# Decode attention beside a gated feed-forward: each tile of keys, values and query weights loaded as two halves from two queues

## The chip, the cores and the metric

The kernel runs on one core of one Trainium2 chip. The metric is device time in microseconds (us) of one execution, as the median of several runs. The core has five engines, each with its own instruction stream: TensorE (PE in the profile; PEld is its loading of weights), VectorE (DVE), ScalarE (ACT), GpSimd (POOL) and SyncE (SP). Memory transfers are issued from the instruction stream of an engine and carried out by 16 DMA engines. The engines wait for one another, and for transfers, by semaphores; a transfer adds 16 to its semaphore when it is complete.

## The reference

For one new token in each of four sequences, the output mixes an attention block over a cache of 4096 positions with a gated feed-forward block. All arrays are float32.

```python
# x: 4 x 1 x 512; k_cache, v_cache: 4 x 32 x 4096 x 128; wq: 512 x 4096; wo: 4096 x 512
# w_gate, w_up: 512 x 1792; w_down: 1792 x 512; gate_w: 512
g = sigmoid((x * gate_w).sum(-1, keepdims=True))

q = (x @ wq).reshape(4, 1, 32, 128).transpose(0, 2, 1, 3)
scores = einsum("bhqd,bhkd->bhqk", q, k_cache) * 128 ** -0.5
p = softmax(scores)
o = einsum("bhqk,bhkd->bhqd", p, v_cache)
a = o.transpose(0, 2, 1, 3).reshape(4, 1, 4096) @ wo

b = (gelu(x @ w_gate) * (x @ w_up)) @ w_down
return g * a + (1 - g) * b
```

Each element of the two caches is used once; together they are 536.9 MB of the 564.7 MB that the kernel reads.

## The kernel before, in words

**Tiles.** The caches are cut into 32 tiles each (`NT`), one for each group of four heads and each sequence. A tile is 128 partitions x 16384 floats: `heads` (L121) gives each partition 128 successive positions of one head, one contiguous row of 64 KB. There are two buffers for keys, `K[0]` and `K[1]`, and one for values, `V`. Before the first tile of values, `V` holds the queries' weights `wq`, also as 128 rows of 64 KB.

**Loads.** The helper `load` (L125) issues every transfer from SyncE, so that they all stand in one queue in the order in which SyncE reaches them. At the start these are `wq`, `x`, the gate's weights and the first two tiles of keys. Then SyncE waits for `wq_done` (L293), the end of the query projection, and loads the first values. After that (L309 to L314) it waits in turn for `summed[i]`, when VectorE has read the tile of keys `i` for the last time, and loads keys `i + 2`; and for `at_values[i]`, when TensorE has read values `i`, and loads values `i + 1`. The last values, tile 31 (`L1`), are loaded at L323, behind the two up projections' weights `w_gate` and `w_up` (L320), which go to the buffer `K[0]`, and ahead of `w_down` and part of `wo`, which go to `K[1]`. The last 14 of 32 row blocks of `wo` (`got_w`, L362) take the place of the up weights; SyncE issues them when `have_hT` (L355) says that those are no longer needed.

**Keys.** For each tile `keys(i)` (L266) runs on VectorE: the product of the whole tile with the query `QB` in place (L269), the sum over each 128 (L271), and three short instructions (L273 to L275) that give the negated maximum `NM`.

**ScalarE.** In tile `i` (L299 to L308) ScalarE takes the next query from PSUM (L221), spreads the one after it (L215), computes the exponentials with `weights(i)` (L283: four activations, one per head), waits for `at_values[i]`, and copies the weighted sum from PSUM to `o` (L308).

**TensorE.** One loop over 31 tiles (L253): the spreading of a query, the softmax's totals (L224), a wait for the values' semaphore `sem_v`, from which it takes 16 off again, 64 groups of matmuls against `V` (L231), and the turning of the result (L237). The last tile is written out after the loop (L380 to L391). In between stand the up projections (L338), for which the order of the instructions puts `got_up` ahead of the last values. After it come the down projection and the output projection (L376, L428), and the result is stored (L433).

**Semaphores of the loads.** The two of the keys, `sem_k`, count up over the kernel (16 for each tile that has landed in that buffer); the one of the values is counted back by TensorE.

Of the kernel before, what the change touches and what calls it, by code (L numbers as in the profile page):

```python
# [34 lines left out]
def tile_gated_mix(ctx: ExitStack, tc: tile.TileContext, x, kc, vc, wq, wo, w_gate, w_up, w_down, gate_w, out):  # L35
    nc = tc.nc
# [4 lines left out]
    KC = DM // P  # L41
# [3 lines left out]
    TW = R * D  # L45
    NG = H // HT
    NT = NG * B
# [32 lines left out]
    K = [kv.tile([P, TW], F32, name=f"k{s}") for s in range(2)]  # L80
    V = kv.tile([P, TW], F32, name="v")
# [25 lines left out]
    def semaphore(name):  # L107
        counters.append(ctx.enter_context(nc.semaphore(name)))
        return counters[-1]

    ctx.enter_context(tc.tile_critical(sync_engine=mybir.EngineType.SP))
    SP = Line(nc.sync, None)
    PE = Line(nc.tensor, semaphore("pe"))
    DV = Line(nc.vector, semaphore("dv"))
    AC = Line(nc.scalar, semaphore("ac"))
    PL = Line(nc.gpsimd, semaphore("pl"))
    token_a, token_d = semaphore("token_a"), semaphore("token_d")
    sem_k = [semaphore(f"sem_k{s}") for s in range(2)]
    sem_v = semaphore("sem_v")

    def heads(src, i):  # L121
        g, b = divmod(i, B)
        return src[b, HT * g:HT * g + HT].rearrange("h (p r) d -> (h p) (r d)", p=PH)

    def load(dst, src, sem=None, name=None):  # L125
        sem = sem or semaphore(name)
        nc.sync.dma_start(dst, src).then_inc(sem, 16)  # L127
        return sem, 16

    def load_k(i):  # L130
        load(K[i % 2], heads(kc, i), sem_k[i % 2])

    def load_v(i):
        load(V, heads(vc, i), sem_v)

    got_q = load(V, wq.rearrange("(p c) n -> p (c n)", c=KC), name="got_q")
    x_sb = o[:B]
    got_x = load(x_sb, x.rearrange("b s d -> (b s) d"), name="got_x")
    gw = gs[:B]
    got_g = load(gw, gate_w.rearrange("(o n) -> o n", o=1).to_broadcast([B, DM]), name="got_g")  # L140
    load_k(0)
    load_k(1)

    p0 = PL.do(nc.gpsimd.memset(ident, 0.0))
    PL.wait(p0)
# [56 lines left out]
    for s in range(2):  # L202
# [3 lines left out]
        wq_done = PE.do(u)  # L206
# [6 lines left out]
    def spread_query(i):  # L213
        g, b = divmod(i, B)
        return nc.scalar.activation(QX, QT[:, b, HT * g:HT * g + HT, None].to_broadcast([P, HT, PH]), AF.Copy)  # L215

    def spread():
        return nc.tensor.matmul(qp[:, :D], QX.rearrange("p h k -> p (h k)"), ident, start=True, stop=True)  # L218

    def take_query(i):  # L220
        return AC.do(nc.scalar.activation(QB[i % 2], qp[:, :D], AF.Copy, scale=scale))  # L221

    def totals():
        return nc.tensor.matmul(tot, ones, RS, start=True, stop=True)  # L224

    def values():
        p = PM.rearrange("p r h -> p (r h)")
        n = R // RJ
        for j in range(n):
            c = j % 4  # L230
            t = nc.tensor.matmul(po[32 * c:32 * c + M], p[:, j * M:(j + 1) * M], V[:, j * RJ * D:(j + 1) * RJ * D],  # L231
                                 start=j < 4, stop=j >= n - 4)
        return t

    def turn():
        for j in range(RJ):
            t = nc.tensor.matmul(quo, o[:, j * D:(j + 1) * D], pick[:, j, :], start=j == 0, stop=j == RJ - 1)  # L237
        return t
# [6 lines left out]
    have_QB = {0: take_query(0)}  # L245
    have_QX = AC.do(spread_query(1))

    L1 = NT - 1
# [4 lines left out]
    with nc.tensor.Fori(0, L1):  # L253
        spread().then_inc(PE.sem, 1)
        nc.tensor.wait_ge(token_a, 2).then_inc(token_a, -2)
        nc.tensor.wait_ge(token_d, 1).then_inc(token_d, -1)  # L256
        totals()
        nc.tensor.wait_ge(sem_v, 16).then_inc(sem_v, -16)  # L258
        values().then_inc(PE.sem, 1)
        nc.tensor.wait_ge(token_a, 1).then_inc(token_a, -1)  # L260
        turn().then_inc(PE.sem, 1)
    PE.n += 3 * L1

    summed, have_nm, have_OT = {}, {}, {}

    def keys(i):  # L266
        k = K[i % 2].rearrange("p (r d) -> p r d", d=D)
        DV.wait((sem_k[i % 2], 16 * (i // 2 + 1)), have_QB[i])
        DV.wait(DV.do(nc.vector.tensor_tensor(k, k, QB[i % 2][:, None, :].to_broadcast([P, R, D]), op=OP.mult)))  # L269
        sc = SC[i % 2]  # L270
        summed[i] = DV.do(nc.vector.tensor_reduce(sc, k, axis=AX.X, op=OP.add))  # L271
        DV.wait(summed[i])
        DV.wait(DV.do(nc.vector.tensor_reduce(m1, sc, axis=AX.X, op=OP.max)))  # L273
        DV.wait(DV.do(nc.vector.transpose(mt, m1.to_broadcast([P, 32]))))  # L274
        have_nm[i] = DV.do(nc.vector.tensor_reduce(NM[i % 2], mt, axis=AX.X, op=OP.max, negate=True))  # L275

    def divide(i, at):
        g, b = divmod(i, B)
        DV.wait(at)
        DV.wait(DV.do(nc.vector.reciprocal(ri, tot)))  # L280
        return nc.vector.tensor_tensor(OT[:, b, HT * g:HT * g + HT], quo, ri, op=OP.mult)

    def weights(i):  # L283
        AC.wait(have_nm[i])
        if i:
            AC.wait(at_values[i - 1])
        for h in range(HT):
            s = slice(h * PH, (h + 1) * PH)
            t = nc.scalar.activation(PM[s, :, h], SC[i % 2][s, :], AF.Exp, bias=NM[i % 2][s, :], scale=1.0,  # L289
                                     accum_out=RS[s, h:h + 1])  # L290
        return t

    SP.wait(wq_done)  # L293
    load_v(0)
    for i in range(NT):
        keys(i)
        if i > 0:
            divide(i - 1, at_turn[i - 1]).then_inc(token_d, 1)
        if i < L1:  # L299
            AC.wait(at_spread[i])  # L300
            have_QB[i + 1] = take_query(i + 1)
            if i + 2 < NT:
                spread_query(i + 2).then_inc(token_a, 1)
            else:
                nc.scalar.sem_inc(token_a, 1)
            weights(i).then_inc(token_a, 1)
            AC.wait(at_values[i])
            nc.scalar.activation(o, po, AF.Copy).then_inc(token_a, 1)  # L308
        if i + 2 < NT:  # L309
            SP.wait(summed[i])  # L310
            load_k(i + 2)
        if i + 1 < L1:
            SP.wait(at_values[i])
            load_v(i + 1)  # L314
    have_PM = AC.do(weights(L1))

    f, down = K[0], K[1]
# [2 lines left out]
    got_up = [load(f[:, s * KC * F:(s + 1) * KC * F], a.rearrange("(p c) n -> p (c n)", c=KC), name=f"got_up{s}")  # L320
              for s, a in enumerate((w_gate, w_up))]
    SP.wait(at_values[L1 - 1])
    load_v(L1)  # L323
    SP.wait(summed[L1])
    got_down = load(down[:, :DR * DM], w_down.rearrange("(p i) n -> p (i n)", i=DR), name="got_down")
    got_wo = [load(down[:, (DR + r0) * DM:(DR + r1) * DM], wo_rows[:, r0 * DM:r1 * DM], name=f"got_wo{r0}")
# [34 lines left out]
    for n in PIECES:  # L361
        got_w.append(load(f[:, r0 * DM:(r0 + n) * DM], wo_rows[:, (W1 + r0) * DM:(W1 + r0 + n) * DM],  # L362
                          name=f"got_w{r0}"))
# [16 lines left out]
    PE.wait(have_PM)  # L380
    nc.tensor.wait_ge(token_d, 1)
    totals()
    nc.tensor.wait_ge(sem_v, 16)
    t = PE.do(values())
    AC.wait(t)
    have_o = AC.do(nc.scalar.activation(o, po, AF.Copy))
# [30 lines left out]
    i = 0  # L417
# [42 lines left out]
```

## Time and profile before

| | us |
|---|---|
| median of 3 runs | 1311.73 |
| lowest, highest | 1311.70, 1312.22 |
| the profiled execution, its own time | 1312.45 |
| its span in the profile | 1310.7 |
| busy in it: VectorE | 1142.5 (87%) |
| busy in it: TensorE matmul, weight load | 390.0 (30%), 136.1 (10%) |
| busy in it: ScalarE | 108.7 (8%) |

The profile describes one execution. A page line of a group of instructions reads: line of the kernel, engine, operation, output<-input with sizes, count | busy us, mean ns of one | idle us of the engine just before them, and what ended most of that idle time. In a timeline the columns are the start in us, the duration in us, engine, line, operation, and in brackets the idle time before it with what ended it; "SPq" is SyncE's issuing of a transfer. In the table of stretches the columns are the stretch, its length, the busy us (and the count of instructions) of PE, PEld, DVE, ACT and POOL, TensorE's granted clock, the share of the 16 DMA engines' time that packets fill, and GB/s. Packets are counted to the stretch in which they begin, so that short stretches scatter. The line of digits "DMA" on the page gives that share in tenths, 9 being 90% or more, over 40 equal slices of the span.

### The profile page before, as it was taken

To read this page: it belongs to the slowest core of one execution; us is meant where nothing else is said; L and a number is where in the kernel's file an instruction comes from. 1 tells how busy PE (TensorE), PEld (TensorE's weight loads), DVE (VectorE), ACT (ScalarE), POOL (GpSimd) and SP (SyncE) were. 2 spreads that over 40 slices of the span, in tenths; PEclk is the share of its full clock that TensorE was granted. 3 is DMA by queue.
4 is the path that set the end of the run, shared out by engine and by line. 5 is a ranking of instruction groups with operands and counts; after the bars stand their busy time and mean duration, and the time that the engine had idled before them with its cause. 6 is when DMAs were issued, how large, how long until landed. Compare 5 with 4: busy or idle time off the path is not lost.

```text
span 1310.7 us, 6525 instructions
## 1 busy us (share of the span) xinstructions
PE 390.0 (30%) x2766; PEld 136.1 (10%) x2766; DVE 1142.5 (87%) x263; ACT 108.7 (8%) x360; POOL 0.7 (0%) x6
## 2 busy tenths in 40 slices
PE   2132123333213333312333321233231133332147
PEld 0010001111001111000111100011010011100012
DVE  1799999999989899998989989998998999899850
ACT  0000111000000000000000000000000000000010
POOL 0000000000000000000000000000000000000000
PEclk9665566666556666656666655666655666665578
DMA  9999999999999999999999999999999999999998
GB/s 417 416 447 428 436 443 422 444 420 448 426 438 438 426 444 420 448 422 442 436 428 444 420 444 424 440 438 428 446 420 444 422 442 436 428 448 418 434 430 342
DMA packets 10846, 564.80 MB, mean 431 GB/s; under 512 B 1212, under 2 KB 1228, under 8 KB 1620
## 3 DMA queue, kind: packets, MB, share of 16 engines
q1 hardware_dynamic: 10836, 564.69, 99.5%
q8 instruction: 4, 0.07, 0.0%
q14 instruction: 6, 0.05, 0.0%
HBM read 564.67 MB, written 0.01 MB: 431 GB/s over the span
## 4 chain that ended last, share of the span: by engine, by line
DMA 51%; DVE 48%; PE 1%; issue 0%; SPq 0%; ACT 0%
DMA k<-in_A_k_cache 45%; DVE k L269 24%; DVE SC L271 24%; DMA k<-in_B_w_up 3%; DMA k<-in_A_wo 3%; PE bank L338 0%; PE bank L428 0%; SPq L127 0%; DVE m L273 0%; DVE k L354 0%; DVE mt L274 0%; DVE k L351 0%; DVE k L352 0%; DVE nm L275 0%; ACT k L349 0%
## 5 line engine op out<-in xcount | busy, mean ns | idle before, releaser
L269 DVE TENSOR_TENSOR k<-k,QB 128x16384 f32<-128x16384 f32 x32 | 551.2, 17225 | 82.6 <-DMA k<-in_A_k_cache 82.6
L271 DVE TENSOR_REDUCE SC<-k 128x128 f32<-128x16384 f32 x32 | 551.0, 17220 | 1.1
L231 PE MATMUL bank<-v,PM 128*16 128x512 f32 x2048 | 294.7, 740 | 569.8 <-PEq L258 555.7
L231 PEld LDWEIGHTS bank<-v,PM 128*16 128x16 f32 x2048 | 69.4, 113 | 768.5 <-issue 754.3
L224 PE MATMUL bank<-RS,ones 128*128 128x4 f32 x64 | 17.7, 347 | 288.0 <-PEq L256 288.0
L308 ACT ACTIVATE o<-bank 128x512 f32<-128x512 f32 x31 | 18.5, 597 | 869.2 <-PE bank L231 869.2
L289 ACT ACTIVATE PM<-SC,nm 32x128 f32<-32x128 f32 x128 | 66.0, 516 | 200.9 <-DVE nm L275 199.4
L224 PEld LDWEIGHTS bank<-RS,ones 128*128 128x128 f32 x64 | 15.8, 306 | 294.3 <-issue 294.3
L237 PE MATMUL bank<-pick,o 128*128 128x4 f32 x256 | 32.9, 252 | 25.1 <-PEq L260 25.1
L237 PEld LDWEIGHTS bank<-pick,o 128*128 128x128 f32 x256 | 31.0, 191 | 53.6 <-issue 52.7
L280 DVE RECIPROCAL ri<-bank 128x4 f32<-128x4 f32 x32 | 5.5, 173 | 22.5 <-PE bank L237 22.5
L289 ACT ACTIVATION_READ_ACCUMULATOR PM<-SC,nm 32x1 f32 x128 | 25.1, 196 | 0.0
L167 DVE COPY xT<-bank 128x32 f32<-128x32 f32 x4 | 0.5, 182 | 21.5 <-PE bank L163 21.5
L218 PE MATMUL bank<-ident,QX 128*128 128x128 f32 x64 | 15.0, 316 | 1.5 <-ACT QX L215 1.5
L221 ACT ACTIVATE QB<-bank 128x128 f32<-128x128 f32 x32 | 8.9, 278 | 47.3 <-PE bank L218 47.3
L432 DVE COPY res<-bank 128x128 f32<-128x128 f32 x1 | 0.3, 292 | 12.5 <-PE bank L428 12.5
L273 DVE TENSOR_REDUCE m<-SC 128x1 f32<-128x128 f32 x32 | 9.2, 286 | 1.1
L215 ACT ACTIVATE QX<-QT 128x128 f32<-128x128 f32 x32 | 9.9, 308 | 2.4 <-DVE QT L209 1.6
L209 DVE COPY QT<-bank 128x16 f32<-128x16 f32 x8 | 0.9, 180 | 10.5 <-PE bank L205 10.5
L218 PEld LDWEIGHTS bank<-ident,QX 128*128 128x128 f32 x64 | 9.7, 192 | 1.9 <-ACT QX L215 1.1
L193 PE MATMUL bank<-v,xT 128*32 128x512 f32 x64 | 9.5, 760 | 0.0
L338 PE MATMUL bank<-k,xT 128*32 128x448 f32 x64 | 8.1, 659 | 2.6 <-DMA k<-in_B_w_up 2.6
(57 smaller groups left out, 63.5 us busy)
## 6 DMA issues: line engine op xcount, KB each, us to landing
k<-in_B_w_gate SPq DMA_DIRECT2D x1, 3584.0 KB, 31.9
k<-in_B_w_up SPq DMA_DIRECT2D x1, 3584.0 KB, 40.0
k<-in_B_w_down SPq DMA_DIRECT2D x1, 3584.0 KB, 29.5
k<-in_A_wo SPq DMA_DIRECT2D x1, 2560.0 KB, 35.2
k<-in_A_wo SPq DMA_DIRECT2D x1, 2048.0 KB, 39.6
k<-in_A_wo SPq DMA_DIRECT2D x2, 1024.0 KB, 33.5
k<-in_A_wo SPq DMA_DIRECT2D x1, 768.0 KB, 35.9
k<-in_A_k_cache SPq DMA_DIRECT2D x32, 42.7
```

The costliest lines, as they stand in the source:

```text
L193: t = nc.tensor.matmul(PO[s][32 * j:32 * j + 32], xT[:, c, :], w[:, c, n0:n0 + HB * D], start=c == 0, stop=c == KC - 1)
L215: return nc.scalar.activation(QX, QT[:, b, HT * g:HT * g + HT, None].to_broadcast([P, HT, PH]), AF.Copy)
L218: return nc.tensor.matmul(qp[:, :D], QX.rearrange("p h k -> p (h k)"), ident, start=True, stop=True)
L221: return AC.do(nc.scalar.activation(QB[i % 2], qp[:, :D], AF.Copy, scale=scale))
L224: return nc.tensor.matmul(tot, ones, RS, start=True, stop=True)
L231: t = nc.tensor.matmul(po[32 * c:32 * c + M], p[:, j * M:(j + 1) * M], V[:, j * RJ * D:(j + 1) * RJ * D], start=j < 4, stop=j >= n - 4)
L237: t = nc.tensor.matmul(quo, o[:, j * D:(j + 1) * D], pick[:, j, :], start=j == 0, stop=j == RJ - 1)
L269: DV.wait(DV.do(nc.vector.tensor_tensor(k, k, QB[i % 2][:, None, :].to_broadcast([P, R, D]), op=OP.mult)))
L271: summed[i] = DV.do(nc.vector.tensor_reduce(sc, k, axis=AX.X, op=OP.add))
L273: DV.wait(DV.do(nc.vector.tensor_reduce(m1, sc, axis=AX.X, op=OP.max)))
L289: t = nc.scalar.activation(PM[s, :, h], SC[i % 2][s, :], AF.Exp, bias=NM[i % 2][s, :], scale=1.0, accum_out=RS[s, h:h + 1])
L308: nc.scalar.activation(o, po, AF.Copy).then_inc(token_a, 1)
```

## The change

Each tile of keys and values, and the queries' weights, is loaded by two transfers into the same buffer: the left half of each of the 128 rows (8192 floats, 32 KB) from SyncE, the right half from ScalarE. Both add to the same semaphore, so the waits go from 16 to 32. ScalarE's half of the first values waits for `wq_done` like SyncE's. In tile `i`, ScalarE issues its half of keys `i + 2` behind the exponentials of tile `i`, and its half of values `i + 1` behind the copy to `o`. Its half of the last values is thereby issued in the loop (`i = 30`), while SyncE's stays behind the up weights at L323 of the kernel before. All other loads stay with SyncE.

```diff
--- before.py
+++ after.py
@@ -127,19 +127,26 @@
         nc.sync.dma_start(dst, src).then_inc(sem, 16)
         return sem, 16
 
-    def load_k(i):
-        load(K[i % 2], heads(kc, i), sem_k[i % 2])
-
-    def load_v(i):
-        load(V, heads(vc, i), sem_v)
-
-    got_q = load(V, wq.rearrange("(p c) n -> p (c n)", c=KC), name="got_q")
+    def half(engine, dst, src, sem):
+        s = slice(0, TW // 2) if engine is nc.sync else slice(TW // 2, TW)
+        engine.dma_start(dst[:, s], src[:, s]).then_inc(sem, 16)
+
+    def load_k(engine, i):
+        half(engine, K[i % 2], heads(kc, i), sem_k[i % 2])
+
+    def load_v(engine, i):
+        half(engine, V, heads(vc, i), sem_v)
+
+    got_q = semaphore("got_q"), 32
+    for engine in (nc.sync, nc.scalar):
+        half(engine, V, wq.rearrange("(p c) n -> p (c n)", c=KC), got_q[0])
     x_sb = o[:B]
     got_x = load(x_sb, x.rearrange("b s d -> (b s) d"), name="got_x")
     gw = gs[:B]
     got_g = load(gw, gate_w.rearrange("(o n) -> o n", o=1).to_broadcast([B, DM]), name="got_g")
-    load_k(0)
-    load_k(1)
+    for i in range(2):
+        for engine in (nc.sync, nc.scalar):
+            load_k(engine, i)
 
     p0 = PL.do(nc.gpsimd.memset(ident, 0.0))
     PL.wait(p0)
@@ -255,7 +262,7 @@
         nc.tensor.wait_ge(token_a, 2).then_inc(token_a, -2)
         nc.tensor.wait_ge(token_d, 1).then_inc(token_d, -1)
         totals()
-        nc.tensor.wait_ge(sem_v, 16).then_inc(sem_v, -16)
+        nc.tensor.wait_ge(sem_v, 32).then_inc(sem_v, -32)
         values().then_inc(PE.sem, 1)
         nc.tensor.wait_ge(token_a, 1).then_inc(token_a, -1)
         turn().then_inc(PE.sem, 1)
@@ -265,7 +272,7 @@
 
     def keys(i):
         k = K[i % 2].rearrange("p (r d) -> p r d", d=D)
-        DV.wait((sem_k[i % 2], 16 * (i // 2 + 1)), have_QB[i])
+        DV.wait((sem_k[i % 2], 32 * (i // 2 + 1)), have_QB[i])
         DV.wait(DV.do(nc.vector.tensor_tensor(k, k, QB[i % 2][:, None, :].to_broadcast([P, R, D]), op=OP.mult)))
         sc = SC[i % 2]
         summed[i] = DV.do(nc.vector.tensor_reduce(sc, k, axis=AX.X, op=OP.add))
@@ -290,8 +297,9 @@
                                      accum_out=RS[s, h:h + 1])
         return t
 
-    SP.wait(wq_done)
-    load_v(0)
+    for line in (SP, AC):
+        line.wait(wq_done)
+        load_v(line.engine, 0)
     for i in range(NT):
         keys(i)
         if i > 0:
@@ -304,14 +312,18 @@
             else:
                 nc.scalar.sem_inc(token_a, 1)
             weights(i).then_inc(token_a, 1)
+            if i + 2 < NT:
+                AC.wait(summed[i])
+                load_k(nc.scalar, i + 2)
             AC.wait(at_values[i])
             nc.scalar.activation(o, po, AF.Copy).then_inc(token_a, 1)
+            load_v(nc.scalar, i + 1)
         if i + 2 < NT:
             SP.wait(summed[i])
-            load_k(i + 2)
+            load_k(nc.sync, i + 2)
         if i + 1 < L1:
             SP.wait(at_values[i])
-            load_v(i + 1)
+            load_v(nc.sync, i + 1)
     have_PM = AC.do(weights(L1))
 
     f, down = K[0], K[1]
@@ -320,7 +332,7 @@
     got_up = [load(f[:, s * KC * F:(s + 1) * KC * F], a.rearrange("(p c) n -> p (c n)", c=KC), name=f"got_up{s}")
               for s, a in enumerate((w_gate, w_up))]
     SP.wait(at_values[L1 - 1])
-    load_v(L1)
+    load_v(nc.sync, L1)
     SP.wait(summed[L1])
     got_down = load(down[:, :DR * DM], w_down.rearrange("(p i) n -> p (i n)", i=DR), name="got_down")
     got_wo = [load(down[:, (DR + r0) * DM:(DR + r1) * DM], wo_rows[:, r0 * DM:r1 * DM], name=f"got_wo{r0}")
@@ -380,7 +392,7 @@
     PE.wait(have_PM)
     nc.tensor.wait_ge(token_d, 1)
     totals()
-    nc.tensor.wait_ge(sem_v, 16)
+    nc.tensor.wait_ge(sem_v, 32)
     t = PE.do(values())
     AC.wait(t)
     have_o = AC.do(nc.scalar.activation(o, po, AF.Copy))
```

## The prediction

> **What bounds the kernel now.** First the page of the profile: the transfers by slice and by queue, the chain that ended last, the costliest groups, the DMA issues.
>
> ```profile
> DMA  9999999999999999999999999999999999999998
> q1 hardware_dynamic: 10836, 564.69, 99.5%
> DMA 51%; DVE 48%; PE 1%; issue 0%; SPq 0%; ACT 0%
> L269 DVE TENSOR_TENSOR k<-k,QB 128x16384 f32<-128x16384 f32 x32 | 551.2, 17225 | 82.6 <-DMA k<-in_A_k_cache 82.6
> L271 DVE TENSOR_REDUCE SC<-k 128x128 f32<-128x16384 f32 x32 | 551.0, 17220 | 1.1
> k<-in_B_w_down SPq DMA_DIRECT2D x1, 3584.0 KB, 29.5
> k<-in_A_wo SPq DMA_DIRECT2D x1, 2560.0 KB, 35.2
> k<-in_A_wo SPq DMA_DIRECT2D x1, 2048.0 KB, 39.6
> ```
>
> One queue (q1) carries 564.69 MB, and its packets fill 99.5% of 16 engines' span. VectorE's two passes over a tile of keys cost 17.2 us each and it still idles 82.6 us for keys. The chain's halves (DMA 51%, DVE 48%) alternate, so the next view is the table of stretches: does any stretch leave the DMA engines free? Its last columns are TensorE's clock, the DMA share and GB/s.
>
> ```profile
> 2.50:42.50 40.00, 12.67 (x82) 4.77 (x82) 3.30 (x19) 2.51 (x8) 0.00 (x0) 0.99 0.98 425
> 42.50:218.70 176.20, 44.50 (x304) 15.49 (x304) 175.40 (x29) 13.12 (x44) 0.00 (x0) 0.61 1.00 434
> 218.70:1218.70 1000.00, 288.45 (x1976) 100.42 (x1976) 919.79 (x183) 84.19 (x285) 0.00 (x0) 0.62 1.00 434
> 1218.70:1259.00 40.30, 13.95 (x106) 4.56 (x106) 36.30 (x12) 3.49 (x12) 0.00 (x0) 0.65 1.00 433
> 1259.00:1268.00 9.00, 5.23 (x34) 1.50 (x34) 4.09 (x7) 2.95 (x9) 0.00 (x0) 0.76 0.93 402
> 1268.00:1304.50 36.50, 22.46 (x216) 7.40 (x216) 1.92 (x8) 1.19 (x2) 0.00 (x0) 0.78 0.98 417
> ```
>
> From 42.5 to 1259 us the share is 1.00 at 433 to 434 GB/s, even to 218.7 us, where VectorE is never idle and it sets the pace of the keys. So the transfers decide from the first load to the last: the bytes are fixed, and the time is bytes over pace plus the ends. The chain in order of time (start, us, what) gives the period:
>
> ```profile
> 2.12 40.43 DMA k<-in_A_k_cache
> ...
> 218.67 38.18 DMA k<-in_A_k_cache
> ...
> 1064.13 42.74 DMA k<-in_A_k_cache
> ...
> 1141.40 42.75 DMA k<-in_A_k_cache
> ...
> 1219.04 40.00 DMA k<-in_B_w_up
> ...
> 1268.66 35.86 DMA k<-in_A_wo
> ...
> 1304.57 2.80 PE bank L428 x48
> ```
>
> From 1064.13 to 1141.40 is 77.27 us for two tiles of keys and two of values, 38.64 a pair. A tile is 128 x 16384 x 4 bytes = 8.389 MB, a pair 16.78 MB: 434 GB/s again. A key load is issued 42.75 us before it lands, though it needs 19.3 us itself: it queues 23.4 us behind other loads. That queue is the cover for all that follows.
>
> **The change part by part.** It removes no byte. (1) Each of 65 tiles (32 of keys, 32 of values, the queries' weights) goes as 32 KB half rows instead of 64 KB rows: at 128 rows over 16 engines, 16 instead of 8 rows per engine and tile, 65 x 8 = 520 more for each engine. (2) 65 more loads, each with its completion. (3) Half of each tile arrives through ScalarE's queue, so the engines serve two queues by turns. (4) ScalarE's loads are issued at other moments than SyncE's. (5) In the tail ScalarE's half of the last values overtakes part of the weights.
>
> Rows and completions (1, 2) have a price in the tail, where landings can be read from whoever waited for them:
>
> ```profile
> 1259.09 4.91 PE L338 MATMUL bank<-k,xT 128*32 128x448 f32 x32 [2.60 <-DMA k<-in_B_w_up]
> ...
> 1278.46 9.90 PE L231 MATMUL bank<-v,PM 128*16 128x512 f32 x64 [14.15 <-DMA v<-in_A_v_cache]
> ...
> 1297.82 1.90 PE L376 MATMUL bank<-k,ow 128*4 128x512 f32 x16 [0.80 <-DMA k<-in_A_wo]
> ...
> 1300.42 1.08 PE L428 MATMUL bank<-k,o 128*32 128x128 f32 x32 [0.69 <-DMA k<-in_A_wo]
> ...
> 1302.78 1.08 PE L428 MATMUL bank<-k,o 128*32 128x128 f32 x32 [1.06 <-DMA k<-in_A_wo]
> ...
> 1304.57 2.76 PE L428 MATMUL bank<-k,o 128*32 128x128 f32 x48 [0.71 <-DMA k<-in_A_wo]
> ```
>
> The last tile of values, one load of 64 KB rows, took 1278.46 - 1259.09 = 19.37 us. The next 8192 KB, the same bytes (3584 + 2560 + 2048), came as three loads with rows of 28, 20 and 16 KB, 24 rows per engine instead of 8, in 1297.82 - 1278.46 = 19.36 us. Sixteen more rows and two more completions cost -0.01 us; reading each difference to 0.04 us, that is -3 to +2 ns a row, -1.6 to +1.0 us for 520. I take +0.5 us: a row cannot well have a negative price, and the measured one is nil. The far bound is the first of the last loads: 1.049 MB in 1300.42 - 1297.82 = 2.60 us, where 19.37 us per tile gives 2.42; 0.18 us over 8 rows is 22 ns a row, 12 us for 520. The two after it make most of that good (2.36 and 1.79 us): the three together take 6.75 us for 2.884 MB, 0.09 us too long over 24 rows, 4 ns a row or 2 us for 520.
>
> The Trainium skill, "DMA: Bandwidth & Descriptors", section "Why small descriptors are slow", states a fixed cost of about 3 cycles for each packet; at the 850 MHz that the same page gives the fabric, the estimate is 3.5 ns x 520 = 1.8 us, and the sum by it 1313.5 us. The two intervals of 19.37 and 19.36 us do not show such a cost, so the measurement decides.
>
> Two queues (3) are nowhere in this trace: all the tiles come through q1. Per turn from one queue to the other, 16 x 65 = 1040 per engine, I bound the price by the same rows: below by -4 ns (a turn that hides what a row costs), above by 22 ns, so -4 to +23 us. I take 0, since successive rows and loads of one queue, the nearest thing to a turn, cost nothing.
>
> The moments (4). ScalarE's key load stands behind the four exponentials, its value load behind the copy of the output:
>
> ```profile
> 1173.68 0.33 SPq L127 DMA_DIRECT2D v<-in_A_v_cache  x1
> 1173.68 0.60 ACT L308 ACTIVATE o<-bank 128x512 f32<-128x512 f32 x1 [29.38 <-PE bank L231]
> ...
> 1175.82 0.28 ACT L221 ACTIVATE QB<-bank 128x128 f32<-128x128 f32 x1 [1.54 <-PE bank L218]
> ...
> 1180.09 0.33 SPq L127 DMA_DIRECT2D k<-in_A_k_cache  x1
> ...
> 1182.80 0.19 ACT L289 ACTIVATION_READ_ACCUMULATOR PM<-SC,nm 32x1 f32 x1
> 1184.17 17.22 DVE L269 TENSOR_TENSOR k<-k,QB 128x16384 f32<-128x16384 f32 x1 [3.04 <-DMA k<-in_A_k_cache]
> ```
>
> SyncE issues the keys at 1180.09; ScalarE would at 1183.0, 2.9 us later. The queue then holds the tile that lands at 1184.17 and 19.3 us of values behind it, so the late half still joins 20 us before its turn. The values are issued at 1173.68 by SyncE and 1174.3 by ScalarE, with keys under way until 1184.17: 9.9 us to spare. Each issue occupies ScalarE 0.33 us. The one after the copy ends at 1174.6, before the 1175.82 at which ScalarE is next released (L221), and the copy's signal to TensorE precedes it; the one after the exponentials is followed by a wait of tens of us for the values. Cost 0. Without these covers ScalarE's queue would run dry, by 0.6 us a tile for values and 2.9 us for keys; even then SyncE's half would take the engines alone, as one queue does now at share 1.00. Only both queues dry at once cost time. Early, the margins are thinner:
>
> ```profile
> 0.91 1.28 ACT L178 ACT_TABLE_LOAD   x1 [0.91 <-SPq L111]
> ...
> 38.45 0.33 SPq L127 DMA_DIRECT2D v<-in_A_v_cache  x1
> 77.08 0.33 SPq L127 DMA_DIRECT2D k<-in_A_k_cache  x1
> ```
>
> A table load of 1.28 us may stand ahead of ScalarE's first loads; the first values are issued by ScalarE behind its query work, some 3 us after 38.45, while two tiles of keys last until 42.55 + 19.3 = 61.9; and the third keys come from SyncE at 77.08, from ScalarE about when the first values land, 61.9 + 19.3 = 81.2. ScalarE's queue is empty there for a few us and its halves then trail, but SyncE's has work. Cost 0.
>
> The tail (5). SyncE's order stays: the up weights, its half of the last values, the down weights, the rest.
>
> ```profile
> 1251.57 0.33 SPq L127 DMA_DIRECT2D v<-in_A_v_cache  x1
> ...
> 1267.54 0.25 DVE L355 TENSOR_TENSOR hT<-k,gates 128x56 f32<-128x56 f32 x1
> ```
>
> ScalarE's half is issued near 1252.2 and shares the engines with the up weights, which have 6.9 us to go: they land near 1266 instead of 1259.09. L355, whose end frees the buffer for the last loads, moves from 1267.8 to 1274.7; they are wanted when the queue ahead of them ends, 1297.8, so 23 us remain. All bytes ahead of the last values are the same, so these land at 1278.46 still. Cost 0; beyond 23 us it would count one for one.
>
> The sum: the profiled execution took 1312.45 us, 1.75 outside its span of 1310.7; with +0.5 it is 1312.95. The runs' median, 1311.73, lies 0.72 below that execution, so I forecast **1312.2 us**.
>
> **The rivals.** *The turns cost (slower).* Each engine, at each half row, has to take up the other queue's row. For it: only a single queue is ever seen at 434 GB/s, and there is no idle engine time to absorb anything. Against: row and load boundaries are free. From 2.5 ns a turn (2.6 us) it decides; at 4 ns it gives 1316, at 12 ns 1324, at 22 ns 1335 us.
>
> *The second queue fills gaps (faster).* The shares of 0.98 over 40 us, 0.93 over 9 and 0.98 over 36.5 leave 0.8 + 0.6 + 0.7 = 2.1 us. That alone gives 1309.6, inside no change; with 4 ns more gained at each of the 520 old rows (2.1 us) 1307.5 us. Against: 1000 us at 1.00 and the same pace in every mix of rows. The Trainium skill's same page, "Rules for kernel authors", says that spreading loads over issuing engines does not help bandwidth; by it this case is void and the time 1311.7 us, and no run here shows it yet.
>
> *The halves drift apart (slower).* A tile counts only when both halves are in, so keys land late by the lag, and with one buffer of values both queues could run dry. It decides when the lag exceeds the 9.9 us of cover; the lag seen is about 3 us, and an empty queue hands its share to the other. A lag of 10.5 us, 0.6 past the cover, over 30 tiles would be 18 us: 1330 us.
>
> *The second queue does nothing* (the halves come one after the other): 1312 us, the forecast's time by another road.
>
> **How the numbers follow.** No change by the forecast or its double: 0.50. Turns that cost: 0.32, mostly near 1316 to 1324. Drift: 0.05. Gaps filled beyond 0.2%: 0.13. About 0.2%, 2.6 us, is what a measurement can tell from no change, so: faster 0.13, same 0.50, slower 0.37. The range runs from 1308.5 to 1324 us (12 ns a turn), leaving out about a tenth on each side; the likeliest case's own is 1310 to 1314.
>
> **What would show it.** A second queue with 65 x 4.194 = 272.6 MB and SyncE's with 292.1; packets up by 65 x 128 rows. If right: share 1.00 and 434 GB/s after 42.5 us, still 38.6 us a pair. If turns cost: share 1.00 but GB/s below 433 in every stretch and a longer pair. If halves drift: share under 1.00 and new waits for values. If gaps filled: GB/s above 434. The forecast is wrong if the steady pair moves by more than 0.08 us (32 pairs, 2.6 us).

## The result and the profile after

The changed kernel takes 1317.62 us (median of 4 runs, 1317.33 to 1317.90) against 1311.95 us before: a ratio of 1.0043, 95% interval 1.0026 to 1.0061. It is slower by 5.7 us, and the whole interval lies above the 0.2% that the prediction counts as no change. The profiled execution has a span of 1315.2 us and took 1317.70 us.

The page of the profile after shows that the change does what it says: a second queue, q10, with the 272.6 MB that the prediction names, and 20205 packets where there were 10846. The two queues of loads hold 20196 of them, 9360 more than the one queue before: 65 x 128 rows and 65 x 16 completions, so that a completion counts as a packet too.

```profile
DMA packets 20205, 564.79 MB, mean 429 GB/s; under 512 B 2252, under 2 KB 2268, under 8 KB 2660
## 3 DMA queue, kind: packets, MB, share of 16 engines
q1 hardware_dynamic: 10836, 292.06, 51.5%
q10 hardware_dynamic: 9360, 272.63, 48.1%
```

The table of stretches has two places that differ from before:

```profile
42.50:218.70 176.20, 44.47 (x306) 15.44 (x306) 170.99 (x28) 14.06 (x48) 0.00 (x0) 0.61 0.99 426
218.70:1218.70 1000.00, 285.83 (x1958) 99.10 (x1962) 917.04 (x183) 83.31 (x283) 0.00 (x0) 0.62 1.00 433
...
80.00:82.00 2.00, 0.00 (x0) 0.00 (x0) 1.93 (x3) 0.00 (x0) 0.00 (x0) 0.50 0.01 0
82.00:84.00 2.00, 0.00 (x0) 0.00 (x0) 1.97 (x3) 1.63 (x7) 0.00 (x0) 0.50 0.87 262
```

The first is early: 426 instead of 434 GB/s, and finer stretches find the hole, a share of 0.01 from 80 to 82 us. In the kernel before the same stretch is

```profile
80.00:82.00 2.00, 1.26 (x6) 0.68 (x10) 2.00 (x1) 0.01 (x2) 0.00 (x0) 0.50 1.26 524
```

(over 1, since packets count where they begin). The second is the long steady part: 433 instead of 434 GB/s at the same share of 1.00. Its size comes out of the chain of waits, in which the keys' arrivals repeat:

```profile
1036.48 17.23 DVE k L276
...
1113.93 17.24 DVE k L276
...
1191.38 17.24 DVE k L276
```

77.45 us for two pairs of tiles, where before it was 77.27: 38.725 us a pair against 38.638. Over 32 pairs that is 2.8 us.

Where the hole comes from is seen in the timeline of the start (ACTq is ScalarE's issuing of a transfer):

```profile
0.91 0.41 ACTq L132 DMA_DIRECT2D v<-in_A_wq  x1
...
1.35 0.93 ACTq L132 DMA_DIRECT2D k<-in_A_k_cache  x2
...
2.31 1.28 ACT L185 ACT_TABLE_LOAD   x1 [2.31 <-issue]
...
25.22 0.61 PE L170 MATMUL bank<-ident,o 4*128 4x4 f32 x4 [25.22 <-DMA o<-in_A_x]
...
27.71 0.68 DVE L178 TENSOR_TENSOR gs<-gs,o 4x512 f32<-4x512 f32 x1 [1.36 <-DMA gs<-in_gate_w]
...
41.14 0.33 SPq L132 DMA_DIRECT2D v<-in_A_v_cache  x1
42.51 0.33 ACTq L132 DMA_DIRECT2D v<-in_A_v_cache  x1
...
47.02 17.23 DVE L276 TENSOR_TENSOR k<-k,QB 128x16384 f32<-128x16384 f32 x1 [5.44 <-DMA k<-in_A_k_cache]
...
81.53 0.33 SPq L132 DMA_DIRECT2D k<-in_A_k_cache  x1
...
82.33 0.52 ACT L296 ACTIVATE PM<-SC,nm 32x128 f32<-32x128 f32 x1 [38.26 <-DVE nm L282]
...
82.88 0.33 ACTq L132 DMA_DIRECT2D k<-in_A_k_cache  x1
...
84.27 0.20 ACT L296 ACTIVATION_READ_ACCUMULATOR PM<-SC,nm 32x1 f32 x1
```

The first keys are complete at 47.02 us, though the bytes ahead of them are the same. In the kernel before it is

```profile
42.58 17.22 DVE L269 TENSOR_TENSOR k<-k,QB 128x16384 f32<-128x16384 f32 x1 [3.70 <-DMA k<-in_A_k_cache]
```

4.44 us earlier. In the changed kernel VectorE therefore finishes them at 81.53 instead of 77.08, and only then does SyncE issue the third keys. The list of DMA issues for the first values gives their landing:

```profile
v<-in_A_v_cache SPq DMA_DIRECT2D x1, 4096.0 KB, 39.5
...
v<-in_A_v_cache ACTq DMA_DIRECT2D x1, 4096.0 KB, 38.7
```

SyncE's half, issued at 41.14, landed at 80.6, and ScalarE's, issued at 42.51, at 81.2. From then until 81.53 nothing was in either queue, and the table shows 0 GB/s from 80 to 82 us. In the tail the landings read from TensorE's waits are

```profile
1267.61 5.73 PE L350 MATMUL bank<-k,xT 128*32 128x448 f32 x32 [4.87 <-DMA k<-in_B_w_up]
...
1283.38 8.52 PE L238 MATMUL bank<-v,PM 128*16 128x512 f32 x64 [9.73 <-DMA v<-in_A_v_cache]
...
1302.79 3.01 PE L388 MATMUL bank<-k,ow 128*4 128x512 f32 x16 [2.02 <-DMA k<-in_A_wo]
```

The up weights are 8.5 us later than before, the last values 4.9 and the part of `wo` 5.0: what the tail rearranges is given back by the last values, and the 4.9 us were lost ahead of it. That is the hole (about 2.3 us by the shares: 1.98 + 0.26) and the steady excess (2.6 us up to there).

### The profile page after: what moved, and what is told of

It reads as the page before. It is cut to its first block, busy times and chain, and to the rows that moved or that the text cites. A ratio compares the mean times of both kernels' runs of the same rounds, so it can differ in the third digit from the quotient of the medians.

```text
span 1315.2 us, 6590 instructions
## 1 busy us (share of the span) xinstructions
PE 388.4 (30%) x2766; PEld 135.5 (10%) x2766; DVE 1142.6 (87%) x263; ACT 108.7 (8%) x360; POOL 0.7 (0%) x6
## 2 busy tenths in 40 slices
DMA packets 20205, 564.79 MB, mean 429 GB/s; under 512 B 2252, under 2 KB 2268, under 8 KB 2660
## 3 DMA queue, kind: packets, MB, share of 16 engines
q10 hardware_dynamic: 9360, 272.63, 48.1%
## 4 chain that ended last, share of the span: by engine, by line
DMA 50%; DVE 48%; ACT 1%; PE 1%; SPq 0%; issue 0%
DMA k<-in_A_k_cache 44%; DVE k L276 24%; DVE SC L278 24%; DMA k<-in_B_w_up 3%; DMA k<-in_A_wo 2%; ACT PM L296 1%; PE bank L350 0%; DVE m L280 0%; SPq L127 0%; DVE mt L281 0%; DVE nm L282 0%; PE bank L440 0%; DVE k L366 0%; DVE k L363 0%; DVE k L364 0%
```

## The experiments

The theory for the hole, called A: two queues on one engine take turns packet by packet, and a small packet counts as much as a half row of 32 KB. SyncE's queue alone holds `x` and the gate's weights, 8 KB each, between the queries' weights and the keys. By the theory each is a row and a completion on the same few engines, four packets in all, and for each of them ScalarE's queue moves on by a half row: 32768 bytes at 434/16 = 27.1 GB/s are 1.21 us. For the steady excess there were several candidates: the turns, the smaller rows, the additional completions, and the pitch between half rows.

The table has, for each kernel of this study that keeps the order of the transfers, the rows per engine and the loads for each tile, the start of VectorE's first product, the pair (from the start of the product of the seventh tile to that of the thirty-first, over 24), the pair from the first 14 of these intervals (seventh to twenty-first tile) and the time with its ratio to the kernel before, run on the same chip.

| kernel | rows | loads | queues | first keys us | pair of 24, us | pair of 14, us | median us | ratio, 95% |
|---|---|---|---|---|---|---|---|---|
| before | 8 | 1 | 1 | 42.58 | 38.638 | 38.637 | 1311.95 | |
| changed | 16 | 2 | 2 | 47.02 | 38.725 | 38.724 | 1317.62 | 1.0026 to 1.0061 |
| gate's weights from ScalarE | 16 | 2 | 2 | 42.48 | 38.737 | 38.724 | 1314.58 | 1.0009 to 1.0028 |
| two more small loads | 16 | 2 | 2 | 52.41 | 38.725 | 38.725 | 1323.07 | 1.0067 to 1.0101 |
| both halves from SyncE | 16 | 2 | 1 | 42.47 | 38.752 | 38.726 | 1314.53 | 1.0011 to 1.0030 |
| quarter rows | 32 | 4 | 2 | 45.05 | 38.899 | 38.899 | 1321.37 | 1.0054 to 1.0088 |
| rows only | 16 | 1 | 1 | 42.36 | 38.726 | 38.712 | 1314.10 | 1.0009 to 1.0028 |
| halves that lie together | 16 | 2 | 1 | 42.25 | 38.750 | 38.725 | 1314.56 | 1.0011 to 1.0031 |
| first loads only | 8 | 1 | 1 (start 2) | 47.17 | 38.637 | 38.605 | 1315.37 | 1.0016 to 1.0038 |

The two columns differ because in five of the profiles (gate's weights, both halves from SyncE, rows only, halves that lie together, first loads only) one of the last ten intervals is 0.4 to 0.7 us longer than the rest. With both halves from SyncE it is this one, 39.43 us:

```profile
798.58 17.23 DVE L276 TENSOR_TENSOR k<-k,QB 128x16384 f32<-128x16384 f32 x1 [3.17 <-DMA k<-in_A_k_cache]
...
838.01 17.23 DVE L276 TENSOR_TENSOR k<-k,QB 128x16384 f32<-128x16384 f32 x1 [3.88 <-DMA k<-in_A_k_cache]
```

What causes it was not settled. It is found with one queue and with two, and adds up to 0.03 us to the average of 24, as much as the smallest differences looked for here, so the steady price is read from the 14 intervals ahead of it. (In the last row the first of the 14, 38.10 us, is not yet steady; the other 13 give 38.644.)

**One small load moved.** In the changed kernel, the gate's weights are issued by ScalarE:

```diff
-    got_g = load(gw, gate_w.rearrange("(o n) -> o n", o=1).to_broadcast([B, DM]), name="got_g")
+    got_g = semaphore("got_g"), 16
+    nc.scalar.dma_start(gw, gate_w.rearrange("(o n) -> o n", o=1).to_broadcast([B, DM])).then_inc(got_g[0], 16)
```

> Theory A (a packet, however small, takes a whole turn): x and the gate's weights are two small loads ahead of the keys in SyncE's queue only; each is a row and a completion, and for each of these packets the other queue sends a whole half row of 1.2 us, so that SyncE's keys come 4 x 1.2 = 4.8 us behind on those engines. With one of the two small loads moved to ScalarE's queue both queues have the same number of packets: VectorE starts near 42.6 to 43.5 us instead of 47.02, the DMA share in 80 to 82 us goes from 0.01 to about 1, and the time falls by 2.3 us to 1315.3 us. Rival B (the halves drift because the issue moments differ): VectorE still starts at 47 us, the share stays near 0, 1317.6 us.

Measured 1314.58 us. The stretches of its profile around 80 us, and the start of its keys:

```profile
80.00:82.00 2.00, 1.34 (x6) 0.68 (x10) 2.00 (x1) 0.00 (x0) 0.00 (x0) 0.50 1.20 492
...
42.48 17.23 DVE L277 TENSOR_TENSOR k<-k,QB 128x16384 f32<-128x16384 f32 x1 [3.78 <-DMA k<-in_A_k_cache]
```

The keys are there at 42.48, the hole is gone, and 3.0 us with it (0.7 more than the shares had suggested). Eight kilobytes that changed queues, 8 packets by the page (10828 in q1 and 9368 in q10), did this; the order of all other issues, and what they wait for, stayed. B falls.

**Two more small loads.** In the changed kernel, ahead of the keys in SyncE's queue:

```diff
+    more = [load(gs[32 * s:32 * s + B], gate_w.rearrange("(o n) -> o n", o=1).to_broadcast([B, DM]), name=f"more{s}")
+            for s in (1, 2)]
...
-    DV.wait(got_g, got_x)
+    DV.wait(got_g, got_x, *more)
```

> Two more copies of the gate's weights, 8 KB each, in SyncE's queue ahead of the keys; they are not used. Theory A (each packet takes a turn): four more packets, 4.8 us more lag: VectorE starts near 51.8 us, both queues stand empty 4.8 us longer around 80 to 87 us, 1322.4 us. Rival B (the lag comes from the issue moments): 16 KB more are 0.04 us, start at 47 us, 1317.6 us.

Measured 1323.07 us. Its stretches, the start of its keys and the issue of the third keys:

```profile
80.00:82.00 2.00, 0.00 (x0) 0.00 (x0) 2.00 (x1) 0.00 (x0) 0.00 (x0) 0.50 0.01 0
82.00:84.00 2.00, 0.00 (x0) 0.00 (x0) 2.00 (x1) 0.00 (x0) 0.00 (x0) 0.50 0.00 0
84.00:86.00 2.00, 0.00 (x0) 0.00 (x0) 2.00 (x1) 0.00 (x0) 0.00 (x0) 0.50 0.00 0
86.00:88.00 2.00, 0.00 (x0) 0.00 (x0) 1.90 (x5) 0.29 (x1) 0.00 (x0) 0.50 0.42 115
...
52.41 17.22 DVE L278 TENSOR_TENSOR k<-k,QB 128x16384 f32<-128x16384 f32 x1 [5.37 <-DMA k<-in_A_k_cache]
...
86.91 0.33 SPq L132 DMA_DIRECT2D k<-in_A_k_cache  x1
```

16 KB more delay the keys by another 5.39 us and the third keys' issue by 5.38 (86.91 against 81.53); the empty time grows, and the median is 5.45 us above that of the changed kernel. With 0, 4 and 8 packets ahead on one side the keys come 0, 4.44 and 9.83 us late: 1.1 to 1.2 us a packet, the half row of the other queue.

**Both halves in one queue.** The change with every `nc.scalar` load issued by SyncE, next to its twin:

```diff
-        engine.dma_start(dst[:, s], src[:, s]).then_inc(sem, 16)
+        nc.sync.dma_start(dst[:, s], src[:, s]).then_inc(sem, 16)
...
             load_k(nc.sync, i + 2)
+            load_k(nc.scalar, i + 2)
...
             load_v(nc.sync, i + 1)
+            load_v(nc.scalar, i + 1)
```

> Both half-row loads of each tile from SyncE, one queue. Theory C (the steady excess is the price of 520 more rows and 65 more completions per engine): no lag at the start (VectorE from 42.6 us), but the pair stays at 38.72 us instead of 38.64, 1314.4 us. Rival D (the excess is the turn from one queue to the other): pair 38.64 us, 1312.0 us.

Measured 1314.53 us. Starts of the products of the seventh and thirty-first tile:

```profile
256.42 17.22 DVE L276 TENSOR_TENSOR k<-k,QB 128x16384 f32<-128x16384 f32 x1 [1.34 <-DMA k<-in_A_k_cache]
...
1186.46 17.23 DVE L276 TENSOR_TENSOR k<-k,QB 128x16384 f32<-128x16384 f32 x1 [3.17 <-DMA k<-in_A_k_cache]
```

(1186.46 - 256.42)/24 = 38.752 us, and ahead of the one long interval (798.58 - 256.42)/14 = 38.726: without any second queue the steady excess is all there. D falls. With the same rows and loads, two queues and one have the same pair (38.724 to 38.726 us) and, with the start in order, the same time (1314.58 and 1314.53).

**Quarter rows.** Each queue sends its half as two loads (and the waits go from 32 to 64):

```diff
-        s = slice(0, TW // 2) if engine is nc.sync else slice(TW // 2, TW)
-        engine.dma_start(dst[:, s], src[:, s]).then_inc(sem, 16)
+        for q in (0, 1) if engine is nc.sync else (2, 3):
+            s = slice(q * TW // 4, (q + 1) * TW // 4)
+            engine.dma_start(dst[:, s], src[:, s]).then_inc(sem, 16)
```

> Each queue sends its half of a tile as two loads of quarter rows (16 KB): 1040 more rows and 130 more completions per engine than with halves. Theory C (rows and completions): the pair grows by twice 0.085 us, to 38.89 us, +4.8 us over the run; theory A: a turn is now 0.6 us, so SyncE's lag at the start halves, VectorE starts near 44.8 us and the empty stretch goes; about 1317.6 - 2.3 + 4.8 = 1320 us. Rival D (turns of whole bytes, no price per row): pair 38.72 us, 1315.3 us.

Measured 1321.37 us, 1.4 us over the expectation. The pair is 38.899 us as foreseen. The start answers to A once more:

```profile
45.05 17.22 DVE L277 TENSOR_TENSOR k<-k,QB 128x16384 f32<-128x16384 f32 x1 [5.29 <-DMA k<-in_A_k_cache]
```

2.47 us late, four packets by 0.6 us: the turn is worth what the other queue's row is worth. Some of the hole is left, 287 GB/s from 80 to 82 us where the expectation had it gone.

**Rows or loads.** Three kernels with one queue part the two. The first is the kernel before with 256 rows of 32 KB in one load:

```diff
-        return src[b, HT * g:HT * g + HT].rearrange("h (p r) d -> (h p) (r d)", p=PH)
+        return src[b, HT * g:HT * g + HT].rearrange("h (x r) d -> (h x) (r d)", x=2 * PH)
...
-        load(K[i % 2], heads(kc, i), sem_k[i % 2])
+        load(halves(K[i % 2]), heads(kc, i).rearrange("(a p) n -> p a n", a=2), sem_k[i % 2])
```

(`halves` is the tile seen as 128 x 2 x 8192; the values likewise.)

> The kernel before, one queue and one load for each tile, but each tile of keys and values comes as 256 rows of 32 KB (two for each partition), so that rows double and completions do not; the positions fall to other partitions and heads, so the output is not the reference's. Theory R (the excess is a price of each row, 5.4 ns): pair 38.725 us instead of 38.64, 1314.5 us. Theory L (the excess is a price of each load with its completion, 43 ns on each engine): pair 38.64 us, 1311.8 us.

Measured 1314.10 us, and from its timeline

```profile
256.66 17.23 DVE L272 TENSOR_TENSOR k<-k,QB 128x16384 f32<-128x16384 f32 x1 [1.69 <-DMA k<-in_A_k_cache]
...
798.63 17.23 DVE L272 TENSOR_TENSOR k<-k,QB 128x16384 f32<-128x16384 f32 x1 [3.10 <-DMA k<-in_A_k_cache]
...
1186.08 17.23 DVE L272 TENSOR_TENSOR k<-k,QB 128x16384 f32<-128x16384 f32 x1 [3.13 <-DMA k<-in_A_k_cache]
```

38.726 us a pair over all 24, and (798.63 - 256.66)/14 = 38.712 ahead of the long interval, with no load more than before. The rows have most of the price: 38.712 - 38.637 = 0.075 us over 16 more rows of each engine, 4.7 ns a row. The rest, up to 38.725, comes with the second load of each tile. With their loads, the quarter rows give (38.899 - 38.724)/32 = 5.5 ns a row, the half rows (38.724 - 38.637)/16 = 5.4.

The second takes the same rows in two loads, so that each load reads 4 MB that lie together:

```diff
+    def block(engine, dst, src, sem):
+        h = 0 if engine is nc.sync else 1
+        nc.sync.dma_start(dst[:, h * TW // 2:(h + 1) * TW // 2], src[h * P:(h + 1) * P]).then_inc(sem, 16)
```

> One queue, two loads for each tile of 128 rows of 32 KB as with the half rows, but each load reads 4 MB that lie together in memory instead of every other 32 KB; the positions fall to other partitions and heads, so the output is not the reference's. Theories R and L both: pair 38.725 us, 1314.5 us. Theory S (the excess is the pitch of 64 KB between rows of 32 KB): pair 38.64 us, 1311.8 us.

Measured 1314.56 us, pair 38.725 (38.750 over 24). Against 38.726 with every other 32 KB, the pitch costs nothing and S falls; against 38.712 with one load, an additional load with its completion costs (38.725 - 38.712)/2, between 0.006 and 0.007 us. For 65 loads that is 0.4 us; the medians differ by as much (1314.56 and 1314.10), within their intervals.

The third was meant to double the loads alone, with 64 whole rows in each:

```diff
-        s = slice(0, TW // 2) if engine is nc.sync else slice(TW // 2, TW)
-        nc.sync.dma_start(dst[:, s], src[:, s]).then_inc(sem, 16)
+        s = slice(0, P // 2) if engine is nc.sync else slice(P // 2, P)
+        nc.sync.dma_start(dst[s], src[s]).then_inc(sem, 16)
```

> One queue, each tile as two loads of 64 whole rows of 64 KB: loads and completions double, the rows stay 128. Theory L: pair 38.725 us, 1314.5 us. Theory R: pair 38.64 us, 1311.8 us. Neither foresees more; if 64 rows are spread worse over the engines than 128, the pair grows well past both.

Measured 2688.99 us, twice the time. It says nothing on L, but much on the form of the split. The steady stretch:

```profile
200.00:1200.00 1000.00, 133.61 (x912) 46.11 (x912) 446.34 (x86) 37.66 (x132) 0.00 (x0) 0.55 1.00 207
```

The DMA engines count as fully busy and move half.

**The start alone.** The kernel before, with halves from two queues for the queries' weights and the first two tiles of keys only:

```diff
+    for engine in (nc.sync, nc.scalar):
+        half(engine, V, wq.rearrange("(p c) n -> p (c n)", c=KC), got_q[0])
...
-    load_k(0)
-    load_k(1)
+    for i in range(2):
+        for engine in (nc.sync, nc.scalar):
+            half(engine, K[i], heads(kc, i), sem_k[i])
```

> The kernel before with the change in its first loads alone: the queries' weights and the first two tiles of keys as halves from two queues, all other tiles whole from SyncE. Theory A (the small loads' packets take turns, SyncE's first keys come late, the queue is dry when the third keys are issued): VectorE starts at 47.0 us, the DMA share in 80 to 82 us is near 0, pair 38.64 us, and the time is before + 3.0 (the change less the kernel with the gate's weights on ScalarE, 1317.62 - 1314.58), 1314.8 us. Rival: the start costs nothing by itself, since all the bytes still flow, 1311.8 us.

Measured 1315.37 us: 3.7 us over its kernel before (1311.67), the pair as before, and

```profile
80.00:82.00 2.00, 0.00 (x0) 0.00 (x0) 1.93 (x2) 0.00 (x0) 0.00 (x0) 0.50 0.00 0
...
47.17 17.23 DVE L276 TENSOR_TENSOR k<-k,QB 128x16384 f32<-128x16384 f32 x1 [5.72 <-DMA k<-in_A_k_cache]
```

Six half loads out of 130 bring more than half of the loss.

**Whole tiles in two queues.** If rows are the steady price and turns are free, whole tiles might use a second queue without loss. The kernel before, with the values issued by ScalarE:

```diff
             nc.scalar.activation(o, po, AF.Copy).then_inc(token_a, 1)
+            if i + 1 < L1:
+                load_v(nc.scalar, i + 1)
...
-        if i + 1 < L1:
-            SP.wait(at_values[i])
-            load_v(i + 1)
```

> The kernel before, all tiles whole (64 KB rows, one load each), with the values (all but the last tile) issued by ScalarE instead of SyncE: two queues without smaller rows. Theory R (rows are the steady price, turns are free and hide a completion): as long as one queue has work nothing is lost, pair 38.61 to 38.64 us, 1311 to 1312 us. Rival: keys and values now share the engines instead of following each other, so each value tile takes up to 38.6 us in place of 19.3, comes late for TensorE, and the one buffer of values makes the pair longer: 40 us or more, 1355 us.

Measured 1458.86 us (ratio 1.1103 to 1.1143): the rival was right in kind and far too low. From its list of waits (who waited for whom: us in total, times, longest):

```profile
DVE ri L280 <- PE bank L237: 231.7, 28, 22.1
```

Before, VectorE waited there once, for 22.5 us, at the end. The pair is 43.9 us, and from 200 to 1200 us the share of the DMA engines is 0.90 at 385 GB/s. What the trace shows is the wait: TensorE waits longer for the values (811.4 us in all, 555.7 before), VectorE, which divides by the total of the last tile before it goes on, waits for TensorE, and the next keys are issued later. That the values come later because keys and values stand side by side in the engines, and not in one order, is the rival's reasoning and was not tested apart.

**64 rows from two queues.** Last, whether the half pace of 64-row loads goes away when the other 64 partitions are loaded beside them. The changed kernel with

```diff
-        s = slice(0, TW // 2) if engine is nc.sync else slice(TW // 2, TW)
-        engine.dma_start(dst[:, s], src[:, s]).then_inc(sem, 16)
+        s = slice(0, P // 2) if engine is nc.sync else slice(P // 2, P)
+        engine.dma_start(dst[s], src[s]).then_inc(sem, 16)
```

> The same split as in the run with 64 whole rows a load (2689 us from one queue), but partitions 0 to 63 from SyncE and 64 to 127 from ScalarE. Theory P (a load of 64 partitions writes to half of the memory's ports, so the pace is halved by where it writes, while all engines count as busy): with both halves in flight both sides are written, the pace comes back to 400 GB/s or more, 1311 to 1420 us. Rival E (the half pace is that of the engines on such a load): 207 GB/s again, 2689 us.

Measured 2617.14 us, 212 GB/s in the steady stretch: P as it was put falls. What in such a load halves the pace stays open.

No kernel tried here beats the one before.

## Why the prediction was right and wrong

The range, 1308.5 to 1324, held the time. The likeliest case, no change, did not come. The range reached as far as the measured time because of the rival of costly turns, but turns were not what cost it: that it held is in part luck.

*What bounds the kernel* stood: the transfers from end to end, bytes over pace. Every loss is either empty queues or a slower pace.

*Rows and completions (1, 2)* were mis-sized: taken at +0.5 us, measured at 2.4 us for the rows alone (1314.10 - 1311.67, interval 1.2 to 3.7) and by the pairs (32 x 0.075); with the additional loads it is 2.8 us (32 x 0.087). The failing step is "reading each difference to 0.04 us": 16 more rows and two more completions cost 0.087 us, and the two intervals of 19.37 and 19.36 us did not show it. The same landings in the run with rows only:

```profile
1261.13 4.86 PE L341 MATMUL bank<-k,xT 128*32 128x448 f32 x32 [3.27 <-DMA k<-in_B_w_up]
...
1280.51 9.26 PE L234 MATMUL bank<-v,PM 128*16 128x512 f32 x64 [14.20 <-DMA v<-in_A_v_cache]
...
1299.93 1.90 PE L379 MATMUL bank<-k,ow 128*4 128x512 f32 x16 [1.50 <-DMA k<-in_A_wo]
```

There the same weights take 19.42 us where they took 19.36, and the last values with twice the rows 19.38 where they took 19.37: one interval between two landings is uncertain by about what was looked for. Why the weights' rows seemed free before was not settled. An average over many pairs is steadier, but the kernel before has tiles with rows of one size only; the 4 ns from its three last loads, which the text had and set aside, was the better guide.

The rule of the Trainium skill on the page "DMA: Bandwidth & Descriptors", section "Why small descriptors are slow", which the prediction set aside, is a fixed cost for each packet. The runs bear out a fixed cost, and give 4.7 ns a row where the prediction's estimate from about 3 cycles was 3.5 ns.

*Two queues (3)*: the price of nil was right. With equal rows and loads, two queues and one have the same pair, 38.724 and 38.726 us, and the same time. The reason given for it, that rows and loads cost nothing, did not hold, so here too the size is right in part by luck.

*The moments (4)* failed at "Cost 0" for the start. The text had found the thin place, the third keys issued about when the first values land, and named the condition, "both queues dry at once". But it let only ScalarE's queue be late there, and took 77.08 us for SyncE's issue as given. That moment hangs on the landing of the first keys, and so on the packets ahead of them in both queues, which the text left out of its working: 8 KB are nothing in bytes, but `x` and the gate's weights are four turns. The price is 3.0 us (1317.62 - 1314.58), or 3.7 us with the start alone. The *drift* rival had the mechanism, with its place and its price wrong: it looked in the steady part, where the cover of 9.9 us was never used up. With 2.8 us for the rows and loads the parts make 5.8 to 6.5 us of the 5.7 measured.

The same section of moments was too careful elsewhere: ScalarE issues its keys 1.35 us behind SyncE (82.88 against 81.53), not 2.9, and its table load stands behind its first loads.

*The tail (5)* was right in that it costs nothing: the up weights land late and the last values take the place they had. The delay was smaller than foreseen, 8.5 us by the trace of which 4.9 are inherited and 3.6 its own, where the text had 6.9.

*The signs to look for* did their work: the pair moved by 0.087 us, over the 0.08 at which the forecast was to be given up, at a share of 1.00; and the early stretch lost pace.

## What to carry to other kernels

Where the transfers already fill the engines, a second queue adds no bandwidth, and the smaller rows that it brings cost pace; look for the price in an average over many periods, not in one interval, and look at the periods one by one before you trust the average: one long interval among 24 was worth as much as the smaller of the two prices found here. When two queues share the engines, count the packets ahead of what is needed first, not the bytes: here a small load in one queue only let the other run ahead by one of its rows for each packet. And when an arrival moves, follow it to the next issue that waits on it, up to the point where the queue would run empty.

## What the runs showed of the hardware

Between two queues the unit of a turn is the packet, here one row: 1.1 to 1.2 us for each small packet beside 32 KB rows and 0.6 us beside 16 KB rows. The Trainium skill, "DMA: Bandwidth & Descriptors", section "Queues, rings and completion order", states turns by packets, and the runs agree.

A row of 32 KB cost 4.7 ns of an engine's time beyond its bytes (38.712 against 38.637 us a pair), and an additional load with its completion 6 to 7 ns (38.725 against 38.712). Rows and loads together, it is 5.4 ns a row from 64 to 32 KB and 5.5 from 32 to 16 KB.

Loads of 64 partitions by 64 KB ran at 207 GB/s from one queue and 212 from two, with all engines counted as busy, where 128 partitions run at 434.

ScalarE's issue of the keys began at 82.88 us, while its exponentials, which stand ahead of it in the program, ran on until 84.47: issuing a transfer did not wait for the activations before it to end.
